# A read-back ring that takes its longest-unused place, one weight part a step earlier, and two splits moved ahead of weight conversions

## The chip, the cores and the metric

The kernel runs on one core of a Trainium2 chip. The metric is the device time of one execution in microseconds (us). Three timed runs of the kernel before gave 1104.66, 1105.78 and 1107.44 us, a median of 1105.78. The profile shown here is of a separate execution, which took 1105.05 us.

## The reference

An attention block with a computed position bias feeds two feed-forward layers. All data is fp32.

```python
attn  = softmax(q @ k.T / 8 + bias)          # 4 batches, 8 heads, 576 positions, head size 64
x     = attn @ v                             # 2304 tokens x 512
h     = x @ w_in;  x = (h - tanh(h)) @ w_out             # layer 0: 512 -> 2048 -> 512
h     = x @ w_in2; out = (s * relu(h)**2 + b) @ w_out2   # layer 1, the same sizes
```

## The kernel before

One core does the work of all 2304 tokens. PE multiplies, ACT (ScalarE) and DVE (VectorE) work on PSUM and SBUF tiles, POOL (GpSimd) does the elementwise work that is left, and SP issues nearly all DMAs. Each engine and SP's queue takes its instructions strictly in the order in which the program wrote them; an instruction that waits holds up all that stand behind it on its engine.

To keep fp32 accuracy every operand of a layer's product is a pair: a rounded high part (an ACT copy) and the low rest (a DVE or POOL subtraction). A product of two pairs is three matmuls. The program splits a hidden tile into such a pair in `split` (L383: ACT copy L385, DVE subtraction L386).

The program has these stages:

- The bias table, and then attention, up to about 280 us of the profile. The layer weights begin to be fetched and converted here.
- The chunk of layer 0: 512 tokens, in 16 steps n, one for each 128 rows of the hidden layer (loop at L839). Step n splits the hidden tile of step n-1, forms the first product of step n (`gemm1`, L369, 12 matmuls, into one of two PSUM tiles h), applies the gate (ACT L377, DVE L378) and adds the second product of step n-2 (`gemm2`, L610, 12 matmuls). So the first product of step n can't start before the split of step n-2 has read its tile h. Beside this, `weights_tick` converts two weights a step in a chain of POOL (L141), ACT (L142), DVE (L147, L152), ACT (L158) and POOL (L97). A list `xq` of small pieces prepares the tokens of the first block (ACT L769, DVE L772 and L775).
- Five blocks (`SUPER`, numbered q = 0 to 4; blocks 0 and 1 are of layer 0, the rest of layer 1). A block handles two column halves at once with a seven-product scheme: sums of weight quarters (`combine`, POOL L724), their split into pairs (`part`, three ACT casts L732 and four POOL subtractions L97) and the products (L912). In the first half-pass (eight steps p) a block forms the first products and adds the second products of one column half; in the second half-pass (16 turns, L999) it adds those of the other half, 12 matmuls (L610) a turn, from the second-layer weights alone.

The second-layer weights of layer 0 are 16 tiles of 512 KB, one for each f. They are kept in DRAM (`wsp_d`) and read back during blocks 0 and 1 through a ring of five SBUF places, w11 to w15 (`NR = 5`). The use order is fixed: each block uses f = 0 to 15 in its first half-pass and f = 15 to 0 in its second. That gives 64 turns, 0 to 63; block 1's second half-pass is turns 48 to 63. The plan of read-backs is made before the blocks are emitted (L676 to L684). Where a turn needs a tile that is in no place, the place whose tile is used again latest is overwritten; tiles that are never used again all have the same key, and Python's `max` then takes the first place of the dictionary:

```python
def next_use(x):
    return turns.index(ring_f[x], n) if ring_f[x] in turns[n:] else len(turns)
x = 16 - NR + n if n < 3 else max(ring_f, key=next_use)
```

`stream` (L686) emits a read-back (DMA L690) as soon as the turn that last uses the place has been emitted and one more turn begun, or at the latest at the turn that needs it. The DMA then waits on SP until PE is done with the place. Between the read-backs of block 1's second half-pass stand the DMAs of `renew` (L696), which fetch the 16 second-layer weights of layer 1, 256 KB each, for block 2.

Of the kernel before, what the change touches and what calls it, by code (L numbers as in the profile page):

```python
# [63 lines left out]
def tile_kernel(ctx, tc, qk, vd, wcat, wts, sb, ltab, psib, ipsi8, out):  # L64
# [55 lines left out]
    def fetch_more(ahead):  # L120
        while (k := len(fetched)) < min(32, wdone[1] + ahead) and all(j < wdone[1] for j in range(k) if fetched[j] == raw_tag(k)):
            fetch(k)
# [52 lines left out]
    def weights_tick():  # L175

        a, b_, c = wdone
        if c < b_:
            both(c)
            wdone[2] += 1  # L180
        if b_ < a:
            high(b_)
            low(b_)
            wdone[1] += 1
        if a in raw_w:
            begin(a, raw_w.pop(a))
            wdone[0] += 1
# [42 lines left out]
    with ExitStack() as c0:  # L230
# [62 lines left out]
        for n in range(NG + 2):  # L293
            if n < NG:
# [3 lines left out]
                for g in range(4 * G, 4 * G + 4):  # L298
                    hid = hids[g] = hp_.tile([128, LW], F32, tag="h", name="hid")
                    k = min(range(2), key=lambda k: held[k] + HC[k][0] + HC[k][1] * nd)  # L300
# [58 lines left out]
    def gemm1(c, f):  # L359
        layer, _, cn = CHUNKS[c]  # L360
        w = wt[layer * 16 + f, 0]
        h = hpool[0].tile([128, CH], F32, tag="h", name="h")[:, 0:cn]
        k = 0
        for kk in range(KD):
            wh = w[:, 0, kk * 128:kk * 128 + 128]
            wl_ = w[:, 1, kk * 128:kk * 128 + 128]
            xh, xl = x_t[c, kk]
            for a, x in ((wh, xh), (wh, xl), (wl_, xh)):
                nc.tensor.matmul(h, a, x, start=(k == 0), stop=(k == 3 * KD - 1))  # L369
                k += 1  # L370
        h_t[c, f] = h

    def gate(c, f):
        layer, _, cn = CHUNKS[c]
        h = h_t.pop((c, f))
        t = ring(F32)[:, 0:cn]
        nc.scalar.activation(out=t, in_=h, func=(AF.Tanh, AF.Relu)[layer])  # L377
        nc.vector.tensor_tensor(out=h, in0=h, in1=t, op=(ALU.subtract, ALU.mult)[layer])  # L378
        if layer:
            nc.vector.tensor_scalar(out=h, in0=h, scalar1=sb_t[:, 0:1], scalar2=sb_t[:, 1:2], op0=ALU.mult, op1=ALU.add)  # L380
        g_t[c, f] = (h, ring(F32R)[:, 0:cn], ring(F32R)[:, 0:cn])

    def split(c, f):  # L383
        g, gh, gl = g_t[c, f]
        nc.scalar.copy(gh, g)  # L385
        nc.vector.tensor_tensor(out=gl, in0=g, in1=gh.bitcast(F32), op=ALU.subtract)  # L386
# [209 lines left out]
    with ExitStack() as cb:  # L596
# [24 lines left out]
        def gemm2(c, f):  # L621
            layer, c0, cn = CHUNKS[c]
            _, gh, gl = g_t.pop((c, f))
            for d in range(KD):
                if f == 0:
                    acc[d] = ps_a.tile([128, 512], F32, tag=f"a{d}", name=f"a{d}")[:, 0:cn]
                accumulate(layer, acc[d], wt[f, 1], gh, gl, d, f == 0, f == NF - 1)
            if f == NF - 1:
                for d in range(KD):
                    leave(acc[d], layer, d, c0)  # L630
# [45 lines left out]
        turns = [f for _ in range(FIRST1) for f in (*range(NF), *reversed(range(NF)))]  # L676
        back, ring_f = [], {f: f for f in range(16 - NR, 16)}
        for n, f in enumerate(turns):
            if f not in ring_f.values():
                def next_use(x):  # L680
                    return turns.index(ring_f[x], n) if ring_f[x] in turns[n:] else len(turns)
                x = 16 - NR + n if n < 3 else max(ring_f, key=next_use)
                back.append((n, f, x, max([k for k in range(n) if turns[k] == ring_f[x]], default=-1)))
                ring_f[x] = f  # L684

        def stream(used):  # L686
# [18 lines left out]
        def load_w(q, p):  # L705
            if p >= NF // 2:
                q, p = q + 1, p - NF // 2
            if q < len(SUPER):
                if (q, p) not in wf_t:
                    wf_t[q, p] = place(f"w{4 - p}" if q == 0 and p < 2 else f"st{(p + 1) % 2}", [2, 512])  # L710
                nc.sync.dma_start(out=wf_t[q, p], in_=win_d[SUPER[q][0], 2 * p:2 * p + 2].rearrange("f p n -> p f n"))

        def combine(q, p):
            if p >= NF // 2:
                q, p = q + 1, p - NF // 2
            if q == len(SUPER):
                return
            w = wf_t[q, p]
            a11, a12, a21, a22 = (w[:, j // 2, j % 2 * 256:j % 2 * 256 + 256] for j in range(4))
            sums_ = sums_at[q, p] = place("XB", [4, 256])  # L720
            s2, s3, s1, s4 = (sums_[:, j] for j in range(4))
            for o, a, b, op in ((s1, a21, a22, ALU.add), (s2, s1, a11, ALU.subtract), (s3, a11, a21, ALU.subtract),
                                (s4, a12, s2, ALU.subtract)):
                nc.gpsimd.tensor_tensor(out=o, in0=a, in1=b, op=op)  # L724

        def part(q, p):
            w, sums_ = wf_t.pop((q, p)), sums_at.pop((q, p))
            cs = cs_t[q, p] = place(f"C{(p + q) % 2}", [7, 2, 256], F32R)
            groups = ((slice(4, 6), w[:, 0].rearrange("p (o n) -> p o n", o=2)), (slice(6, 7), w[:, 1:2, 256:512]),
                      (slice(0, 4), sums_))  # L730
            for o, x in groups:
                nc.scalar.copy(cs[:, o, 0], x)  # L732
            for o, x in groups[:2]:
                rest(cs[:, o, 1], x, cs[:, o, 0])
            for k in (0, 2):
                rest(cs[:, k:k + 2, 1], sums_[:, k:k + 2], cs[:, k:k + 2, 0])
# [102 lines left out]
        for n in range(NS):  # L839
            want = min(32, ND + max(0, int(RATE * (n - 2))))  # L840
            if n < 2:
                weights_tick()
            last = [seq[n - 1]] if len(PR) < n <= len(seq) else []
            while wdone[2] < want:
                weights_tick()
                if last:
                    split(*last.pop())
            if last:
                split(*last.pop())
            fetch_more(AHEAD)  # L850
            c, f = seq[n]
            if n >= len(PR):
                gemm1(c, f)
                gate(c, f)
            if n >= LAG:
                gemm2(*seq[n - LAG])
            for _ in range({8: 1, 9: 2, 10: 2, 11: 1, 12: 1, 13: 1, 14: 1, 15: 2}.get(n, 0)):
                xq.pop(0)()
            if n == 6:
                load_w(0, 0)  # L860
            if n == 9:
                combine(0, 0)
            if n == 12:
                part(0, 0)
                load_w(0, 1)
            if n == 14:
                combine(0, 1)
        flush(9)
        for _ in range(3):
            n, f, x, _ = back.pop(0)  # L870
# [210 lines left out]
```

## Time and profile before

| | |
|---|---|
| timed runs, median (lowest, highest) | 1105.78 us (1104.66, 1107.44) |
| profiled execution | 1105.05 us, span 1103.3 us |
| busy in the span | PE 95%, DVE 65%, ACT 53%, POOL 53% |
| mean granted TensorE clock | 0.975 of full speed |
| moved by DMA | 170.48 MB, 155 GB/s over the span |

The span runs from the first to the last instruction of the profiled execution; the 1.75 us between it and that execution's time lie outside the instructions. A line number is that of the kernel before. In a timeline row the first number is the start, the second how long the merged group of instructions lasted, and brackets hold the engine's idle time before it and what ended it. PE's matmuls overlap a little, so that starts, not ends, are compared. A windows row gives a stretch, its length, the busy us (and instructions) of PE, PEld, DVE, ACT and POOL, the granted clock as a share of full speed, the DMA engines' busy share and the GB/s moved. `x_d` stands for the DRAM tensors x1_d and x2_d, since the views leave numbers out of names.

### The profile page before, as it was taken

To read this page: it belongs to the slowest core of one execution; us is meant where nothing else is said; L and a number is where in the kernel's file an instruction comes from. 1 tells how busy PE (TensorE), PEld (TensorE's weight loads), DVE (VectorE), ACT (ScalarE), POOL (GpSimd) and SP (SyncE) were. 2 spreads that over 40 slices of the span, in tenths; PEclk is the share of its full clock that TensorE was granted. 3 is DMA by queue.
4 is the path that set the end of the run, shared out by engine and by line. 5 is a ranking of instruction groups with operands and counts; after the bars stand their busy time and mean duration, and the time that the engine had idled before them with its cause. 6 is when DMAs were issued, how large, how long until landed. Compare 5 with 4: busy or idle time off the path is not lost.

```text
span 1103.3 us, 18821 instructions
## 1 busy us (share of the span) xinstructions
PE 1049.0 (95%) x6664; PEld 846.6 (77%) x6664; DVE 720.7 (65%) x1415; ACT 584.7 (53%) x1208; POOL 589.8 (53%) x786
## 2 busy tenths in 40 slices
PE   9999999999999999999999955589999999999998
PEld 4366666666787799998888844489988999899987
DVE  8888888887487788877777721045565655755552
ACT  8887777777475545545444511045554443634441
POOL 2376777788387588516665300049941663355600
PEclk9999999999999999999999976699999999999999
DMA  7847474731696577685776322141121112021000
GB/s 284 308 159 268 160 262 143 223 133 61 227 366 257 189 274 291 210 286 179 250 249 212 132 96 86 57 144 59 58 86 49 57 50 84 29 86 40 20 29 29
DMA packets 68349, 170.48 MB, mean 155 GB/s; under 512 B 7456, under 2 KB 13728, under 8 KB 68256
## 3 DMA queue, kind: packets, MB, share of 16 engines
q1 hardware_dynamic: 67824, 168.89, 44.2%
q8 instruction: 52, 0.85, 0.3%
q10 hardware_dynamic: 432, 0.39, 0.1%
q14 instruction: 41, 0.34, 0.1%
HBM read 123.22 MB, written 46.04 MB: 153 GB/s over the span
## 4 chain that ended last, share of the span: by engine, by line
PE 76%; DMA 7%; DVE 6%; POOL 2%; issue 2%; ACT 2%; SPq 0%; DVEq 0%; ACTq 0%; POOLq 0%
PE a L610 19%; PE Z L912 8%; PE V L912 8%; PE o L533 6%; PE Y L912 6%; PE s L434 5%; PE X L912 5%; PE Z L610 5%; PE V L610 5%; DMA w<-wsp_d 4%; PE t L478 3%; PE X L610 3%; PE Y L610 2%; PE h L369 1%; POOL pn L472 1%
## 5 line engine op out<-in xcount | busy, mean ns | idle before, releaser
L97 POOL TENSOR_TENSOR C<-st,C 128x512 fp32r<-128x512 f32 x76 | 76.4, 1028 | 206.4 <-ACT C L732 167.3
L472 POOL TENSOR_SCALAR pn<-p,sm 128x576 f32<-128x576 f32 (+2 forms) x224 | 131.8, 605 | 41.4 <-DVE sm L463 37.8
L610 PE MATMUL a<-w,ring 128*128 128x512 f32 x576 | 146.5, 392 | 0.0
L610 PE MATMUL a<-ring,w 128*128 128x512 f32 (+1 forms) x576 | 127.7, 371 | 0.0
L610 PEld LDWEIGHTS a<-w,ring 128*128 128x128 f32 x576 | 107.5, 188 | 20.5
L610 PEld LDWEIGHTS a<-ring,w 128*128 128x128 f32 x576 | 105.8, 188 | 15.0
L441 DVE CUSTOM_DVE_ANT_0 raw<-s,bias 128x576 f32<-128x576 f32 x144 | 103.7, 752 | 17.4 <-PE s L434 15.5
L455 ACT ACTIVATE p<-raw,mn 128x576 f32<-128x576 f32 x144 | 110.9, 775 | 7.6 <-DVE mn L441 5.6
L97 POOL TENSOR_TENSOR C<-XB,C 128x512 fp32r<-128x512 f32 x80 | 107.2, 1363 | 0.0
L912 PE MATMUL Z<-C,C 128*128 128x384 f32 (+1 forms) x480 | 102.0, 346 | 1.1 <-DVE ring L825 0.7
L533 PE MATMUL o<-pt,vv 128*64 128x256 f32 (+1 forms) x640 | 95.0, 418 | 1.3 <-DVE xo L540 1.3
L434 PE MATMUL s<-qk 64*128 64x288 f32 (+1 forms) x640 | 91.6, 429 | 2.4 <-DVE mn L441 1.3
L912 PEld LDWEIGHTS Z<-C,C 128*128 128x128 f32 x480 | 85.4, 188 | 6.5 <-DVE ring L825 1.7
L434 PEld LDWEIGHTS s<-qk 64*128 64x128 f32 (+1 forms) x640 | 47.0, 175 | 43.3 <-DVE mn L441 18.8
L141 POOL TENSOR_SCALAR s<-w 128x512 f32<-128x512 f32 x60 | 48.4, 809 | 58.0 <-DMA w<-in_wts 25.8
L724 POOL TENSOR_TENSOR XB<-st 128x256 f32<-128x256 f32 x76 | 61.0, 802 | 19.5 <-DMA st<-win_d 17.4
L610 PE MATMUL X<-ring,w 128*128 128x384 f32 (+1 forms) x96 | 31.8, 447 | 38.0 <-DMA w<-wsp_d 38.0
L516 ACT COPY pt<-t 128x512 f32<-128x512 f32 x64 | 37.4, 584 | 45.0 <-PE c L478 28.6
L478 PEld LDWEIGHTS t<-ident,pn 64*128 64x128 f32 x1184 | 51.8, 139 | 9.3 <-DVE pt L516 1.5
L809 ACT ACTIVATE ring<-Y 128x384 f32<-128x384 f32 (+1 forms) x40 | 20.5, 513 | 70.7 <-PE Y L912 40.2
L533 PEld LDWEIGHTS o<-pt,vv 128*64 128x64 f32 x640 | 38.9, 136 | 24.1 <-DVE xo L540 1.7
L809 ACT ACTIVATE ring<-X 128x384 f32<-128x384 f32 (+1 forms) x40 | 20.5, 513 | 69.1 <-DVE X L931 35.6
(167 smaller groups left out, 2323.6 us busy)
## 6 DMA issues: line engine op xcount, KB each, us to landing
w<-in_wts SPq DMA_DIRECT2D x60, 512.0 KB, 4.9
w<-wsp_d SPq DMA_DIRECT2D x47, 512.0 KB, 4.7
st<-win_d SPq DMA_DIRECT2D x38, 512.0 KB, 3.8
qk<-in_qk SPq DMA_DIRECT2D x16, 864.0 KB, 5.8
bias_d<-m SPq DMA_DIRECT2D x36, 296.0 KB, 3.8
bias<-bias_d SPq DMA_DIRECT2D x32, 288.0 KB, 4.6
win_d<-s SPq DMA_DIRECT2D x32, 256.0 KB, 5.7
wsp_d<-w SPq DMA_DIRECT2D x16, 512.0 KB, 6.6
```

What stands on the lines that cost most here:

```text
L97: nc.gpsimd.tensor_tensor(out=lo, in0=raw, in1=hi.bitcast(F32), op=ALU.subtract)
L141: nc.gpsimd.tensor_scalar(out=sg, in0=hw, scalar1=0.0, scalar2=1.0, op0=ALU.mult, op1=ALU.mult)
L434: nc.tensor.matmul(o[0:n, c, 0:288], q[h, ee, t * 128:t * 128 + n], kk[h, ee], start=True, stop=True)
L441: nc.vector.tensor_tensor_reduce(out=raw.rearrange("p (c j) -> p c j", c=2), in0=s_t.pop((x, j))[:, :, 0:288], in1=bias_t[pairs[i][0], k]. ...
L455: nc.scalar.activation(out=p, in_=raw, func=AF.Exp, scale=-1.0, bias=mn, accum_out=sm[:, j:j + 1])
L472: nc.gpsimd.tensor_scalar(out=pn[:, c:c + b - a], in0=p[:, a:b], scalar1=sm[:, j:j + 1], scalar2=0.0, op0=ALU.mult, op1=ALU.add)
L478: nc.tensor.transpose(out_, in_, ident[ROWS[r], ROWS[r]])
L533: nc.tensor.matmul(o[h], v[:, e, j], unit_t[i, u][:, 8 if j == 4 else 4 * e + j, 0:n], start=(j == 0), stop=(j == 4))
L610: nc.tensor.matmul(o, x, y, start=first and j == 0, stop=last and j == 2)
L724: nc.gpsimd.tensor_tensor(out=o, in0=a, in1=b, op=op)
L809: nc.scalar.activation(out=t, in_=c, func=(AF.Tanh, AF.Relu)[layer])
L912: nc.tensor.matmul(o, cs[:, a, l, i * 128:i * 128 + 128], unit(q, u, i, r), start=begins and i == 0 and j == 0, stop=i == 1 and j == 2, sk ...
```

## The change

Three edits, in the order of the diff:

- The ring's key becomes a pair. Among places whose tiles are needed equally late, the one whose tile was last used longest ago is taken. Up to turn 52 no tie decides, so the plan differs only in the last 11 read-backs, turns 53 to 63. Before, all 11 go to w11, and each overwrites the tile used in the turn just before (turn 53: two turns before). Now they go to w15, w14, w12, w11, w13 in rotation, and the tile overwritten was last used five turns earlier (turn 53 takes w15, last used in turn 48).
- `part(0, 0)` and the load `load_w(0, 1)` that follows it move from the end of chunk step 12 to the end of chunk step 11.
- In chunk steps 13, 14 and 15 the split of the step before stands ahead of the step's weight conversions; before, it stood behind the first conversion. (Step 15 has no conversions, so two splits move.)

```diff
         for n, f in enumerate(turns):
             if f not in ring_f.values():
+                def last_use(x):
+                    return max([k for k in range(n) if turns[k] == ring_f[x]], default=-1)
+
                 def next_use(x):
-                    return turns.index(ring_f[x], n) if ring_f[x] in turns[n:] else len(turns)
+                    return turns.index(ring_f[x], n) if ring_f[x] in turns[n:] else len(turns), -last_use(x)
                 x = 16 - NR + n if n < 3 else max(ring_f, key=next_use)
-                back.append((n, f, x, max([k for k in range(n) if turns[k] == ring_f[x]], default=-1)))
+                back.append((n, f, x, last_use(x)))
                 ring_f[x] = f
...
             last = [seq[n - 1]] if len(PR) < n <= len(seq) else []
+            if n > 12:
+                split(*last.pop())
             while wdone[2] < want:
                 weights_tick()
                 if last:
...
-            if n == 12:
+            if n == 11:
                 part(0, 0)
                 load_w(0, 1)
```

In SP's queue during block 1's second half-pass stands, before (`w11` and the like are the SBUF places, `wsp_d` holds the read-back tiles, `wout_d` the weights of layer 1):

```order
L696 DMA w2_8493<-wout_d_72 128x512
L696 DMA w3_8513<-wout_d_72 128x512
L690 DMA w11_8536<-wsp_d_73 128x1024
L696 DMA w4_8538<-wout_d_72 128x512
L690 DMA w11_8558<-wsp_d_73 128x1024
L696 DMA w9_8560<-wout_d_72 128x512
L690 DMA w11_8580<-wsp_d_73 128x1024
```

and now:

```order
L699 DMA w1_8473<-wout_d_72 128x512
L693 DMA w14_8495<-wsp_d_73 128x1024
L699 DMA w2_8497<-wout_d_72 128x512
L693 DMA w12_8517<-wsp_d_73 128x1024
L699 DMA w3_8519<-wout_d_72 128x512
L693 DMA w11_8542<-wsp_d_73 128x1024
L699 DMA w4_8544<-wout_d_72 128x512
```

The read-backs rotate over the places and stand some three fetches of `renew` earlier in the queue; the number of DMAs is the same.

On DVE, from the gate of step 12 to the split of step 13 (tiles h are the hidden tiles, `ring_5685` and `ring_5754` the low parts that the splits write), stands before:

```order
L378 TENSOR_TENSOR h_5668<-h_5668,ring_5681 128x512
L775 TENSOR_TENSOR w5_5450<-w7_5575,w5_5450 128x384
L775 TENSOR_TENSOR w6_5452<-w8_5577,w6_5452 128x384
L147 SCALAR_TENSOR_TENSOR y_5665<-y_5665,s3_5664 128x512
L152 SCALAR_TENSOR_TENSOR s6_5663<-st1_5607,y_5665 128x512
L386 TENSOR_TENSOR ring_5685<-h_5668,ring_5684 128x512
L147 SCALAR_TENSOR_TENSOR y_5722<-y_5722,s2_5721 128x512
L152 SCALAR_TENSOR_TENSOR s0_5720<-w14_5609,y_5722 128x512
L378 TENSOR_TENSOR h_5737<-h_5737,ring_5750 128x512
L772 TENSOR_TENSOR w1_5700<-w5_5450,w1_5700 128x384
L772 TENSOR_TENSOR w2_5702<-w6_5452,w2_5702 128x384
L147 SCALAR_TENSOR_TENSOR y_5734<-y_5734,s3_5733 128x512
```

and now (the low parts are `ring_5695` and `ring_5754`):

```order
L378 TENSOR_TENSOR h_5678<-h_5678,ring_5691 128x512
L778 TENSOR_TENSOR w5_5450<-w7_5575,w5_5450 128x384
L778 TENSOR_TENSOR w6_5452<-w8_5577,w6_5452 128x384
L386 TENSOR_TENSOR ring_5695<-h_5678,ring_5694 128x512
L147 SCALAR_TENSOR_TENSOR y_5675<-y_5675,s3_5674 128x512
L152 SCALAR_TENSOR_TENSOR s6_5673<-st1_5607,y_5675 128x512
L147 SCALAR_TENSOR_TENSOR y_5724<-y_5724,s2_5723 128x512
L152 SCALAR_TENSOR_TENSOR s0_5722<-w14_5609,y_5724 128x512
L378 TENSOR_TENSOR h_5737<-h_5737,ring_5750 128x512
L775 TENSOR_TENSOR w1_5710<-w5_5450,w1_5710 128x384
L775 TENSOR_TENSOR w2_5712<-w6_5452,w2_5712 128x384
L386 TENSOR_TENSOR ring_5754<-h_5737,ring_5753 128x512
```

Each of the two splits moved past one pair L147, L152 of a weight conversion.

On POOL, around the end of step 11 (C0 is the tile that `part(0, 0)` fills, w12 and C3 are weights of the conversion chain), stands before:

```order
L141 TENSOR_SCALAR s3_5603<-st0_5541 128x512
L97 TENSOR_TENSOR w12_5645<-s6_5590,w12_5645 128x512
L141 TENSOR_SCALAR s2_5652<-w13_5543 128x512
L97 TENSOR_TENSOR C3_5530<-s0_5602,C3_5530 128x512
L141 TENSOR_SCALAR s3_5664<-st1_5607 128x512
L97 TENSOR_TENSOR C0_5704<-w4_5336,C0_5704 128x2x256
L97 TENSOR_TENSOR C0_5704<-w4_5336,C0_5704 128x256
L97 TENSOR_TENSOR C0_5704<-XB_5512,C0_5704 128x2x256 x2
```

and now:

```order
L141 TENSOR_SCALAR s3_5603<-st0_5541 128x512
L97 TENSOR_TENSOR C0_5645<-w4_5336,C0_5645 128x2x256
L97 TENSOR_TENSOR C0_5645<-w4_5336,C0_5645 128x256
L97 TENSOR_TENSOR C0_5645<-XB_5512,C0_5645 128x2x256 x2
L97 TENSOR_TENSOR w12_5655<-s6_5590,w12_5655 128x512
L141 TENSOR_SCALAR s2_5662<-w13_5543 128x512
L97 TENSOR_TENSOR C3_5530<-s0_5602,C3_5530 128x512
L141 TENSOR_SCALAR s3_5674<-st1_5607 128x512
```

The four subtractions of the part moved past two links of the conversion chain; on ACT the three casts L732 moved likewise, to directly behind the gate of step 11.

## Rows read from the trace of the kernel before

**Rows 1.** Waits of PE: line, releaser: us in total, times, longest.

```profile
PE X L610 <- DMA w<-wsp_d: 38.0, 11, 4.0
PE h L369 <- DVE ring L386: 4.1, 2, 3.1
```

**Rows 2.** Windows: chunk's last steps, block 0's second half-pass, block 1's unstalled, stalled turns.

```profile
350.62:367.70 17.08, 12.93 (x49) 10.18 (x49) 11.46 (x17) 5.96 (x12) 11.68 (x12) 0.90 0.43 156
466.34:499.78 33.44, 33.44 (x194) 33.44 (x194) 24.83 (x40) 13.84 (x30) 8.13 (x8) 1.00 0.68 237
620.66:634.26 13.60, 13.60 (x61) 11.07 (x59) 9.70 (x16) 5.32 (x11) 5.55 (x6) 1.00 0.50 161
634.26:724.63 90.37, 52.40 (x133) 37.76 (x133) 12.70 (x23) 9.76 (x20) 2.55 (x2) 0.72 0.23 79
```

**Rows 3.** Timeline of PE: block 1's second half-pass, first product of block 2.

```profile
620.66 0.84 PE L610 MATMUL X<-ring,w 128*128 128x512 f32 x3
623.38 0.84 PE L610 MATMUL X<-ring,w 128*128 128x512 f32 x3
...
642.24 1.62 PE L610 MATMUL X<-ring,w 128*128 128x512 f32 x3 [3.84 <-DMA w<-wsp_d]
...
724.63 1.20 PE L912 MATMUL X<-XA,C 128*128 128x384 f32 x6
```

**Rows 4.** Timeline of SP's queue: block 0's read-backs, then one stalled turn's DMAs.

```profile
472.19 17.55 SPq L690 DMA_DIRECT2D w<-wsp_d  x10
...
647.73 0.32 SPq L690 DMA_DIRECT2D w<-wsp_d  x1
648.10 0.42 SPq L696 DMA_DIRECT2D w<-wout_d  x1
```

**Rows 5.** Landing times: of all read-backs (line L690), of the fetches of renew.

```profile
DMA to landing us min/median/max: 3.3/4.7/6.9
...
w<-wout_d SPq DMA_DIRECT2D x16, 256.0 KB, 3.9
```

**Rows 6.** Timeline of PE: first products of steps 14, 15, and block 0's start.

```profile
351.62 3.01 PE L369 MATMUL h<-X,C 128*128 128x512 f32 x12 [1.01 <-DVE ring L386]
...
360.50 4.53 PE L369 MATMUL h<-X,C 128*128 128x512 f32 x12 [3.14 <-DVE ring L386]
...
367.70 1.23 PE L912 MATMUL X<-XA,C 128*128 128x384 f32 x6
...
378.86 0.62 PE L912 MATMUL V<-C,C 128*128 128x384 f32 x2 [0.22 <-DVE C L772]
```

**Rows 7.** Timeline of DVE: splits of steps 12 and 13, what stands between.

```profile
350.88 0.69 DVE L386 TENSOR_TENSOR ring<-h,ring 128x512 fp32r<-128x512 f32 x1 [2.58 <-ACT ring L385]
354.48 0.70 DVE L147 SCALAR_TENSOR_TENSOR y<-y,s 128x512 int32<-128x512 int32 x1 [2.91 <-POOL s L141]
...
356.42 2.10 DVE L772 TENSOR_TENSOR w<-w,w 128x384 fp32r<-128x384 f32 x2
358.44 0.68 DVE L147 SCALAR_TENSOR_TENSOR y<-y,s 128x512 int32<-128x512 int32 x1
...
359.76 0.68 DVE L386 TENSOR_TENSOR ring<-h,ring 128x512 fp32r<-128x512 f32 x1
```

**Rows 8.** Timeline of ACT and POOL: splits' copies, conversion's start, the part.

```profile
341.45 0.95 POOL L141 TENSOR_SCALAR s<-w 128x512 f32<-128x512 f32 x1
...
347.42 0.92 ACT L732 CAST C<-w 128x512 fp32r<-128x512 f32 x2
348.12 2.00 POOL L97 TENSOR_TENSOR C<-w,C 128x512 fp32r<-128x512 f32 x2 [2.23 <-ACT C L732]
...
350.06 2.53 POOL L97 TENSOR_TENSOR C<-XB,C 128x512 fp32r<-128x512 f32 x2
350.27 0.57 ACT L385 CAST ring<-h 128x512 fp32r<-128x512 f32 x1
...
356.54 0.59 ACT L385 CAST ring<-h 128x512 fp32r<-128x512 f32 x1
```

## The prediction

> **What bounds the kernel now.** I read the waits of PE first, since PE is busy 95% of the span. Two of them matter: 38.0 us in 11 waits for read-backs of `wsp_d`, and 4.1 us in 2 waits of a first product for a split [rows 1]. Then the windows, to see what these places cost beside the idle time. In block 1's second half-pass PE runs through its first five turns, 13.60 us of 13.60, and then needs 90.37 us for the other eleven, at a mean granted clock of 0.72, between its two levels of 1.2 and 2.4 GHz; DMA is busy to 0.23 there [rows 2]. The stalls cost more than their idle time: after each the matmuls themselves run slower. Third, the timelines: of PE for the length of a turn, of SP for what is issued when, and of DVE, ACT and POOL at the end of the chunk for why the two splits come late.
>
> **Edit 1, the ring.** It adds and removes no instruction; eleven read-backs get another place, and so another turn to wait for.
>
> An unstalled turn lasts 623.38 - 620.66 = 2.72 us; a stalled one (724.63 - 634.26) / 11 = 8.22 us [rows 2, 3]. The stalled turn is read-back and product in a row: the tile that the read-back overwrites was used in the turn just before, so its DMA can't go until that turn is done, and PE then waits 3.5 to 4 us for it (3.84 at 642.24) and works the rest, some 4.4 us, at the lowered clock.
>
> Now turn 53 overwrites a tile last used in turn 48, turn 54 one of turn 49, and so on: the DMA goes four turns, 4 x 2.72 = 10.9 us, before its tile is wanted. The landing time of all read-backs is 4.7 us in the median and 6.9 at most [rows 5], so 4.0 us of cover are left even for the slowest. Block 0's second half-pass is the nearest row: it has eleven read-backs with the same lead of four turns, its turns are shorter (33.44 / 16 = 2.09 us), ten of its read-backs go out in 17.55 us, and PE is busy 33.44 of 33.44 us at full clock [rows 2, 4].
>
> The queues that the read-backs are moved past: on SP each stands three fetches of `renew` earlier, and the first now stands ahead of the four stores of the finished accumulators. Those stores then start when turn 48 is done, near 623.4, and free the places of their SBUF copies some us later; the first split that such a place holds up is for turn 53, which starts at 634.26, so I cost it at nothing. If that cover were gone, each us of lateness would be a us of PE, once. The fetches of `renew` follow a read-back within 0.4 us, as at 647.73 and 648.10 [rows 4], with no wait of their own, and stay so.
>
> What is late next? Transport: the half-pass moves 161 x 13.60 + 79 x 90.37 = 9.3 MB [rows 2]. In 16 x 2.72 = 43.5 us that is 214 GB/s, under the 237 at which block 0's half-pass kept PE full. In its eleven loaded turns alone, however, a read-back and a fetch are 768 KB in 2.72 us, 289 GB/s; no row of these half-passes shows that. From the near side it costs nothing; from the far side, held to 237 GB/s, a turn would last 3.32 us and the eleven 6.6 us more. I take nothing: the lead of 10.9 us covers a lag that grows by 0.6 us a turn through all eleven but the last. Splits: DVE has 9.70 + 12.70 = 22.4 us of work in the whole half-pass and ACT 15.1 [rows 2], for 43.5 us.
>
> So the half-pass takes 43.5 us instead of 724.63 - 620.66 = 104.0: **-60.4 us**. Block 2 then starts as it does now: its own weights for the first steps are already there, and the last fetches of `renew` still wait for turns 61 to 63.
>
> **Edits 2 and 3, the end of the chunk.** From 350.62 to 367.70 PE has four products of 12 matmuls, 4 x 2.72 = 10.9 us of work, and takes 17.08 at a clock of 0.90 [rows 2]. The 6.2 us between are a wait of 1.0 at step 14, one of 3.14 at step 15, and a product that took 4.53 instead of 3.01 right after it [rows 6].
>
> Step 14 waits for the split of step 12. Its DVE half at 350.88 waited 2.58 us for its ACT half at 350.27, which stood behind the part's casts (from 347.42) and a conversion [rows 7, 8]. Step 15 waits for the split of step 13: its ACT half was done at 357.1, but DVE first did two token pieces (2.10 us) and a conversion pair (from 358.44) and reached it at 359.76 [rows 7, 8].
>
> I follow the new order with these durations. On POOL the part's four subtractions, 2.00 + 2.53 = 4.5 us [rows 8], now stand ahead of a conversion's start that ran at 341.45; it moves to about 345.5 (some of POOL's idle time takes up the rest), and DVE, which waits for it, is about 2.5 us later at the gate of step 12. From there the split of step 12 follows at once, without casts on ACT and conversion on DVE before it: it ends near 351.3, against 351.6 now. The wait at step 14 shrinks by 0.3 us only; what edit 3 gains there, edit 2 takes on POOL. Then the next two conversions find POOL earlier (DVE waited 2.91 us for it at 354.48 [rows 7], which goes), and the split of step 13 comes ahead of one: it ends at 357.0 to 358.0 instead of 360.4. The wait of 3.14 becomes 0 to 0.7, and with it the slow product. Block 0's first product would start at 363 to 364 instead of 367.70. Of these 4 us not all stays: ten us later PE waits for DVE's token pieces (378.86, [rows 6]), and DVE's own chain is only about 3 us earlier.
>
> Bounds: 6.2 us if all of the stretch's loss goes; below nothing, +2.5 us, if the delay by POOL reaches PE and nothing else does. I take **-3.0 us**, near where the replay with the rows' durations ends.
>
> The load behind the part (`load_w(0, 1)`) goes to SP ahead of two stores; nobody waits for either in these rows, so nothing.
>
> **Sum.** 1105.05 - 60.4 - 3.0 = 1041.6 us against the profiled execution. The median of the runs is 0.7 above that execution, so 1042.
>
> **Rivals.**
>
> A: transport sets the pace of the eleven turns. For it, 289 GB/s, which block 0's half-pass doesn't reach; against it, the lead and the DMA share of 0.68 at 237 GB/s. With 6.6 us more: 1049.
>
> B: a split becomes the late one. The DMA wait hid that ACT and DVE had whole turns idle. If each of the eleven turns waits 1 us for its split: 1053. Against it, block 0's half-pass again, where DVE worked 24.83 of 33.44 us and PE never waited.
>
> C: the change doesn't do what it says, because a read-back stands in SP's queue behind a fetch that waits for its own place. Each turn so hit stays at 8.2 us; three of eleven cost 16 us: 1058. Against it, no fetch waited [rows 4].
>
> D: slower. Two DMAs are in effect carried one after the other, and the stall now covers only one of them. A turn then costs a read-back and a fetch in a row, 4.7 + 3.9 = 8.6 us by the medians, and with the longest read-back 6.9 + 3.9 = 10.8 [rows 5]; it decides against the change once the pair takes more than today's 8.2 + 3.0 / 11 = 8.5 us. At 10.8: 11 x 2.6 = 28 us more than now, less 3, gives 1131. For it, the 79 GB/s of the stalled stretch; against it, that stretch moved little because little was asked for, and ten read-backs landing in 4.7 us went out 1.76 us apart without delay [rows 2, 4]. The Trainium skill's page "DMA: Bandwidth & Descriptors", section "Bandwidth", gives the rule that speaks for this rival: batch transfers to 1 MiB or more for three quarters of the peak, so 256 and 512 KB are on its poor side. By that page's cost of about 2.0 us plus bytes over 436 GB/s, read as one transfer after another, a turn would be an estimated 3.2 + 2.6 = 5.8 us and the kernel near 1076, still faster. The 237 GB/s of block 0's half-pass with 512 KB read-backs disagrees with that reading.
>
> **How the numbers follow.** The forecast has 0.84, A 0.09, B 0.03, C 0.02, D 0.02. The forecast's own range comes from the bounds of edits 2 and 3: 1105.8 - 60.4 - 6.2 = 1039 to 1105.8 - 60.4 + 2.5 = 1048. The range is 1038 to 1050, which takes in A at its full price and leaves out B, C and D. A measurement of this kernel can't tell less than 0.3%, 3.3 us, from no change. Every case but D is faster by ten times that; D lies on both sides of it. Faster 0.975, same 0.005, slower 0.02.
>
> **What would show it.** Right: in the waits of PE the row on `wsp_d` is gone or under 2 us; the second half-pass of block 1 is one stretch of 16 equal turns of 2.72 us at a granted clock of 1.0 and about 214 GB/s; the first products of steps 14 and 15 start about 6 us apart, and the second takes 3.0 us. Wrong: turns of 3.3 us with PE waiting for read-backs (A); PE waiting for ACT or DVE on `ring` (B); single turns of 8 us (C); landing times over 8 us (D); for edits 2 and 3, a DVE row L147 that waits for POOL near 344 by more than 2.5 us, or a wait of more than 1 us at step 15.

## The result and the profile after

The changed kernel takes 1039.87 us (median of four runs, 1038.54 to 1040.16). The four runs of the kernel before beside it have a median of 1105.49 us. The ratio is 0.9402 [0.9385, 0.9418], so the change takes off 65.6 us. The profiled execution took 1040.15 us, with a span of 1038.4 us and a mean granted clock of 1.000. PE is busy 99% of the span, DVE 69%, ACT 56%, POOL 57%.

The waits of PE in the changed kernel; the columns are those of [rows 1]:

```profile
PE b L239 <- POOL ident masks.py:199: 1.4, 1, 1.4
...
PE h L369 <- DVE ring L386: 0.9, 1, 0.9
```

The row on `wsp_d`, 38.0 us before, is gone altogether; the largest wait left is of the program's start, far from the change. Windows of the changed kernel, block 1's second half-pass (up to the start of block 2), and from there to the end:

```profile
616.21:659.73 43.52, 43.52 (x193) 36.04 (x192) 23.36 (x39) 15.03 (x30) 8.28 (x8) 1.00 0.71 247
659.73:1038.40 378.67, 374.37 (x1873) 337.63 (x1871) 209.06 (x367) 174.54 (x339) 187.38 (x194) 1.00 0.17 56
```

The first line answers to the last two of [rows 2] together. PE works 43.52 of 43.52 us at the upper clock, 2.4 GHz; before, the same 16 turns took 724.63 - 620.66 = 103.97. The second line is as long as the same stretch before, 1103.30 - 724.63 = 378.67 us: nothing is given back later.

The timeline of PE in the changed kernel: the first two turns of that half-pass and block 2's first product.

```profile
616.21 0.84 PE L610 MATMUL X<-ring,w 128*128 128x512 f32 x3
...
618.93 0.84 PE L610 MATMUL X<-ring,w 128*128 128x512 f32 x3
...
659.73 1.23 PE L917 MATMUL X<-XA,C 128*128 128x384 f32 x6
```

The starts are 2.72 us apart, as in the unstalled turns of [rows 3], now for all 16. The span's 64.9 us are thus 60.45 in the half-pass and 620.66 - 616.21 = 4.45 in its earlier start. Now SP's queue of the changed kernel (start, duration of the issue, line):

```profile
619.13 0.32 SPq L693 DMA_DIRECT2D w<-wsp_d  x1
...
620.23 2.74 SPq L173 DMA_DIRECT2D x_d<-ring  x4
...
623.77 0.57 SPq L693 DMA_DIRECT2D w<-wsp_d  x1
...
632.73 0.32 SPq L693 DMA_DIRECT2D w<-wsp_d  x1
633.10 0.42 SPq L699 DMA_DIRECT2D w<-wout_d  x1
635.45 0.32 SPq L693 DMA_DIRECT2D w<-wsp_d  x1
...
654.49 5.76 SPq L699 DMA_DIRECT2D w<-wout_d  x5
```

The read-back at 619.13 is for turn 53, which starts five turns after 616.21. The next one stood behind the four stores and went out at 623.77, about 2 us late. From 627.29 on a read-back goes out each 2.72 us with a fetch 0.4 us behind it. The last five fetches of `renew` now fall almost wholly into the half-pass. In the kernel before they went out behind it:

```profile
724.83 2.22 SPq L696 DMA_DIRECT2D w<-wout_d  x5
```

Landing times of all read-backs in the changed kernel, then of the eleven in the half-pass alone, in the changed kernel and in the kernel before:

```profile
DMA to landing us min/median/max: 3.5/5.4/7.8
...
DMA to landing us min/median/max: 3.8/4.7/6.6
...
DMA to landing us min/median/max: 3.3/3.5/3.8
```

The eleven lengthened from 3.5 to 4.7 us in the median and from 3.8 to 6.6 at most. A likely reason is that, with the read-backs issued ahead, more is in flight at once. The longest landings of all, 6.9 before [rows 5] and 7.8 now, are of other read-backs. The lead of 10.9 us covers the eleven, and so does the 8.8 us left to the one that went out at 623.77.

Last the chunk's end in the changed kernel: on PE the first products of steps 14 and 15 and the starts of block 0,

```profile
351.11 3.02 PE L369 MATMUL h<-X,C 128*128 128x512 f32 x12 [0.86 <-DVE ring L386]
...
356.70 2.90 PE L369 MATMUL h<-X,C 128*128 128x512 f32 x12
...
362.15 1.23 PE L917 MATMUL X<-XA,C 128*128 128x384 f32 x6
...
372.92 0.62 PE L917 MATMUL Z<-C,C 128*128 128x384 f32 x2 [0.77 <-DVE C L775]
```

and on DVE the conversion that POOL delays, the split of step 12, the token pieces and the split of step 13:

```profile
346.35 0.70 DVE L147 SCALAR_TENSOR_TENSOR y<-y,s 128x512 int32<-128x512 int32 x1 [2.38 <-POOL s L141]
...
350.37 0.69 DVE L386 TENSOR_TENSOR ring<-h,ring 128x512 fp32r<-128x512 f32 x1 [1.06 <-ACT ring L385]
...
354.82 1.10 DVE L775 TENSOR_TENSOR w<-w,w 128x384 fp32r<-128x384 f32 x2
355.84 0.68 DVE L386 TENSOR_TENSOR ring<-h,ring 128x512 fp32r<-128x512 f32 x1
```

The wait at step 14 is 0.86 us instead of 1.01, the one at step 15 is gone and with it the product of 4.53 us [rows 6]. DVE does wait for POOL behind the part's subtractions. The split of step 13 stands directly behind the token pieces. Those took 1.10 us, not 2.10 [rows 7]. Beside them POOL had an operation with one tile as input until 355.04, and then none until 356.13; in the kernel before it had this conversion's subtraction there:

```profile
356.71 1.39 POOL L97 TENSOR_TENSOR w<-s,w 128x512 fp32r<-128x512 f32 x1 [0.40 <-ACT w L158]
```

### The profile page after: what moved, and what is told of

It is laid out like the page before. It is cut to its first block, busy times and chain, and to the rows that moved or that the text cites. A ratio compares the mean times of both kernels' runs of the same rounds, so it can differ in the third digit from the quotient of the medians.

```text
span 1038.4 us, 18818 instructions
## 1 busy us (share of the span) xinstructions
PE 1024.7 (99%) x6664; PEld 832.8 (80%) x6664; DVE 721.6 (69%) x1415; ACT 584.8 (56%) x1208; POOL 592.2 (57%) x786
## 4 chain that ended last, share of the span: by engine, by line
PE 78%; DVE 7%; DMA 4%; POOL 3%; issue 2%; ACT 2%; SPq 0%; DVEq 0%; ACTq 0%; POOLq 0%
PE a L610 20%; PE Z L917 8%; PE V L917 8%; PE o L533 7%; PE s L434 6%; PE Y L917 6%; PE X L917 5%; PE V L610 5%; PE Z L610 5%; PE t L478 3%; PE Y L610 2%; PE X L610 2%; DVE raw L441 1%; POOL pn L472 1%; POOL C L97 1%
## 5 line engine op out<-in xcount | busy, mean ns | idle before, releaser
L478 PE MATMUL t<-ident,pn 64*128 64x64 f32 x1184 | 54.8, 223 | 1.0 <-DVE pt L516 1.0
```

What stands on the lines that cost most here:

```text
L478: nc.tensor.transpose(out_, in_, ident[ROWS[r], ROWS[r]])
```

## The experiments

### Each edit by itself

The ring's key alone, in the kernel before:

```diff
-return turns.index(ring_f[x], n) if ring_f[x] in turns[n:] else len(turns)
+return turns.index(ring_f[x], n) if ring_f[x] in turns[n:] else len(turns), -last_use(x)
```

> The kernel before with the ring's new key alone; the end of the chunk is as before. Theory T (each of the eleven stalled turns shrinks from 8.22 us to PE's own 2.72, and nothing else depends on it): block 1's second half-pass is 43.5 us long, 60.4 less, and the time is 1105.5 - 60.4 = 1045.1 us. The waits for split at the chunk's end, 1.0 and 3.14 us, stay. Rival R (the earlier end of the chunk helps the ring, or the ring's stretch gives back something later): more than 1 us away from 1045.

It took 1043.65 us (1042.41 to 1044.54), 0.9444 [0.9426, 0.9462] of the kernel before: 61.4 us less (59.4 to 63.4). PE with this edit alone, at the end of the chunk and around the half-pass:

```profile
351.57 4.61 PE L369 MATMUL h<-X,C 128*128 128x512 f32 x12 [2.22 <-DVE ring L386]
...
360.44 3.06 PE L369 MATMUL h<-X,C 128*128 128x512 f32 x12 [1.50 <-DVE ring L386]
...
618.43 0.84 PE L610 MATMUL X<-ring,w 128*128 128x512 f32 x3
...
661.95 1.23 PE L915 MATMUL X<-XA,C 128*128 128x384 f32 x6
```

The half-pass is 43.52 us without the other edits, so this one carries the result. The time is 1.45 us under the expected 1045.1, past the 1 us that the rival was given. Its interval covers 60.4 us, though, and the half-pass has the length that the theory says, so the rival isn't shown. In this profile the half-pass starts 620.66 - 618.43 = 2.23 us earlier with no edit ahead of it; so the 4.45 us of the changed kernel are not all the work of edits 2 and 3. The chunk is as in the kernel before, and yet its two waits are 2.22 and 1.50 us where [rows 6] have 1.01 and 3.14, and here the first product is the slow one. Between executions of the same instructions these waits scatter by more than a microsecond.

The part alone, and the splits alone:

```diff
-            if n == 12:
+            if n == 11:
                 part(0, 0)
                 load_w(0, 1)
```

> The kernel before with the part one step earlier and nothing else. Theory T (two causes in a row: the part's casts and a conversion delay the split of step 12, a conversion delays the split of step 13; POOL's four subtractions, moved ahead of the conversion chain, cost DVE about 2.4 us at the gate of step 12, but give the next conversions POOL earlier): the wait at step 14 grows to about 2 us, the one at step 15 shrinks to about 1, so that the slow product after it goes: 1.5 to 3 us faster than before, 1102.5 to 1104. Rival R (the part's move only costs, and the gain is the splits'): the wait at step 15 stays over 3 us and the time is 1105.5 or more.

```diff
+            if n > 12:
+                split(*last.pop())
             while wdone[2] < want:
```

> The kernel before with the two splits ahead of the conversions and nothing else. Theory T: the split of step 12 comes about 1 us earlier, so that the wait at step 14 goes, but POOL still does the part's four subtractions after it, DVE still waits for POOL at 354, and the split of step 13 ends near 359: a wait of about 3 us at step 15 stays, and the slow product with it. 1 to 1.5 us faster than before, 1104 to 1104.5. Rival R (the splits' move alone gives what both give): 4 us faster, 1101.4, no wait at step 15.

The part alone took 1102.48 us (1099.52 to 1105.23), ratio 0.9979 [0.9966, 0.9992]: 2.3 us less (0.9 to 3.8). PE with the part alone, first products of steps 13, 14 and 15:

```profile
346.46 3.02 PE L369 MATMUL h<-X,C 128*128 128x512 f32 x12 [1.03 <-DVE ring L386]
...
354.59 3.01 PE L369 MATMUL h<-X,C 128*128 128x512 f32 x12 [2.39 <-DVE ring L386]
...
360.81 3.03 PE L369 MATMUL h<-X,C 128*128 128x512 f32 x12 [0.48 <-DVE ring L386]
```

And DVE with the part alone:

```profile
348.75 0.70 DVE L147 SCALAR_TENSOR_TENSOR y<-y,s 128x512 int32<-128x512 int32 x1 [2.34 <-POOL s L141]
```

DVE waits 2.34 us for POOL, and behind it step 14 waits 2.39 us, more than in [rows 6]; step 13 waits too, which was not expected. At step 15 the wait shrinks from 3.14 to 0.48.

The splits alone took 1102.32 us (1101.4 to 1105.19), ratio 0.9984 [0.997, 0.9997]: 1.8 us less (0.3 to 3.3). PE with the splits alone, steps 14 and 15, and then DVE's wait for POOL:

```profile
349.97 2.92 PE L369 MATMUL h<-X,C 128*128 128x512 f32 x12
...
357.45 3.04 PE L369 MATMUL h<-X,C 128*128 128x512 f32 x12 [1.84 <-DVE ring L386]
```

```profile
353.84 0.70 DVE L147 SCALAR_TENSOR_TENSOR y<-y,s 128x512 int32<-128x512 int32 x1 [2.69 <-POOL s L141]
```

Step 14 no longer waits, and the wait for POOL at 353.84 stays, as in [rows 7]. Step 15 waits 1.84 us, and the slow product went, which was expected to stay.

Both together (the two diffs above, without the ring):

> The kernel before with the part and the splits moved, the ring as before. Theory T: the two moves together give 4 us or a little more, the difference between the time of the changed kernel and the ring's 60.4: 1105.5 - 4.5 = 1101.0; one wait under 1 us at step 14, none at step 15, full clock in block 0's first products; the eleven stalled turns stay at 8.2 us. Rival R (the difference of 5 us is scatter between runs or comes from the ring): the time stays within 1 us of 1105.5.

1101.78 us (1100.33 to 1106.32), ratio 0.9978 [0.9966, 0.9991]: 2.4 us less (1.0 to 3.8). That is less than the 4 us expected. PE's row on the splits in the profile of this version, an execution of 1106.32 us, the longest of the twelve:

```profile
PE h L369 <- DVE ring L386: 2.2, 2, 1.3
```

Each alone gives about what both give. A likely reason, from the rows above, is that the part's place costs at step 14 what the splits' place gains there. The intervals are too wide to rank the three versions, and the forecast of -3.0 us lies in the last one.

### How much lead a read-back needs

In the changed kernel's key, of the dead tiles the one used most recently, but at least two (or three) turns ago:

```diff
-..., -last_use(x)
+..., (last_use(x) <= n - 2) * (1 + last_use(x))
```

> The changed kernel, but in the last eleven read-backs the place overwritten is one last used two turns earlier (before: one; changed: five). The plan up to turn 52, the number of DMAs and the bytes are the same. Theory T (what counts is the time from the place's release to its next turn against the landing of one read-back): a read-back has one turn, 2.72 us, to land, and a release plus issue plus landing took about 3.8 us in the kernel before. Two read-backs overlap, so a turn takes about (2.72 + 3.8) / 2 = 3.3 us at full clock: PE waits about 0.5 us a turn, eleven turns cost 6 us, and the time is 1046; if the waits lower the clock, up to 1056. Rival R1 (any rotation is enough, since the fault was that only one read-back was under way): within 2 us of the changed kernel's 1039.9. Rival R2 (the pace is set by bytes, not by the lead): also as the changed kernel.

1047.96 us (1046.77 to 1048.47), ratio 0.949 [0.9476, 0.9504]. PE with a distance of two turns: the starts of five turns in a row, and the window from turn 52 to block 2.

```profile
644.20 0.94 PE L610 MATMUL X<-ring,w 128*128 128x512 f32 x3 [0.68 <-DMA w<-wsp_d]
...
647.34 0.93 PE L610 MATMUL X<-ring,w 128*128 128x512 f32 x3
...
651.48 0.94 PE L610 MATMUL X<-ring,w 128*128 128x512 f32 x3 [1.17 <-DMA w<-wsp_d]
...
654.33 0.84 PE L610 MATMUL X<-ring,w 128*128 128x512 f32 x3
...
658.13 0.93 PE L610 MATMUL X<-ring,w 128*128 128x512 f32 x3 [0.92 <-DMA w<-wsp_d]
```

```profile
627.29:667.43 40.14, 34.92 (x145) 26.27 (x144) 15.23 (x27) 11.17 (x22) 2.58 (x2) 1.00 0.56 190
```

Every second turn waits, 0.7 to 1.2 us, and two turns last 6.5 to 7.3 us: about one turn and the landing of a read-back (3.5 us in the median of these eleven), with two read-backs under way in turn. That is 40.14 / 12 = 3.3 us a turn, as expected from the lead; so a rotation of any kind (R1) is not enough. The granted clock stayed at 1.00 through these waits, while the stalls of 3.5 to 4 us had brought the stretch to 0.72 [rows 2].

```diff
-..., -last_use(x)
+..., (last_use(x) <= n - 3) * (1 + last_use(x))
```

> As the run before, with places last used three turns earlier. Theory T: a read-back has two turns, 5.4 us, to land, against a landing of 4.7 us in the median before and 5.4 in the changed kernel: three overlap, (2.72 + 3.8) / 3 = 2.2 us is under PE's 2.72, so no steady wait; single late ones (the longest landing was 7.8 us in the changed kernel) cost some tenths each: 1040 to 1043. Rival R3 (the whole lead of four turns is needed): over 1045.

1039.06 us (1038.69 to 1039.65), ratio 0.9411 [0.9397, 0.9425], which the changed kernel's interval covers. No wait for `wsp_d` is in the profile. Landing times of the eleven at this distance:

```profile
DMA to landing us min/median/max: 3.3/3.7/4.2
```

The DMA goes two turns, 5.44 us, ahead here; that covers even the longest of these landings, and PE waits for none. Two of the change's four turns of lead are spare.

### How far transport is from the pace

The changed kernel with an extra copy of 512 KB inside DRAM, which nothing uses, behind each of the last eleven read-backs:

```diff
+                if len(back) < 11:
+                    nc.sync.dma_start(out=junk_d[len(back)], in_=wsp_d[15 - len(back)])
```

> The changed kernel with one more 512 KB transfer, DRAM to DRAM, behind each of the last eleven read-backs; its result is used by nobody. A loaded turn then moves 1.25 MB (and writes half of it back to DRAM) instead of 768 KB: 482 GB/s at PE's pace. Theory T (bytes set the pace only above what the trace has shown, 365 to 380 GB/s): a turn would need about 3.5 us at 370 GB/s, 0.8 more than PE's, eleven of them 8.8 us; the lead of 10.9 us hides most of the lag that builds up, so PE waits 1 to 5 us in the last of the eleven turns and 1041 to 1046 us result. Rival R4 (transport was close to its limit already, and the changed kernel got by on its lead): 10 us or more slower than the changed kernel, over 1050, with waits from the third or fourth loaded turn on.

1043.53 us (1042.78 to 1046.12), ratio 0.9459 [0.9443, 0.9475], 3.7 us above the changed kernel and 4.5 above the version with a distance of three turns, which ran beside it. PE with the copies, three turns late in the half-pass, and windows of turns 51 to 56 and 57 to 62:

```profile
640.27 0.93 PE L611 MATMUL X<-ring,w 128*128 128x512 f32 x3
...
643.46 0.93 PE L611 MATMUL X<-ring,w 128*128 128x512 f32 x3 [0.21 <-DMA w<-wsp_d]
...
646.67 0.93 PE L611 MATMUL X<-ring,w 128*128 128x512 f32 x3 [0.23 <-DMA w<-wsp_d]
```

```profile
623.95:640.27 16.32, 16.32 (x73) 13.37 (x72) 11.83 (x22) 8.45 (x17) 0.00 (x0) 1.00 1.02 400
640.27:659.43 19.16, 17.92 (x74) 13.04 (x73) 5.57 (x9) 3.11 (x6) 2.58 (x2) 1.00 1.02 416
```

The DMA engines are full, at 400 to 416 GB/s. For six turns the lead still keeps PE at 2.72 us a turn (16.32 / 6); then transport sets 3.2 us a turn. This is what rival A would have looked like; the changed kernel itself, at 247 GB/s, is far from it.

### A second profile of the changed kernel, and the part split in two

The changed kernel again, without an edit:

> The changed kernel once more, beside the next run, so that both share the runs of the kernel before. 1039.9 us, within 1 us; the ratio to the kernel before within 0.938 to 0.942.

1039.86 us (1038.34 to 1042.9), ratio 0.9414 [0.9393, 0.9435]. PE in this second profile (of the execution of 1042.9 us), first products of steps 13 and 14:

```profile
346.85 3.01 PE L369 MATMUL h<-X,C 128*128 128x512 f32 x12 [1.00 <-DVE ring L386]
...
353.90 3.01 PE L369 MATMUL h<-X,C 128*128 128x512 f32 x12 [1.32 <-DVE ring L386]
```

The same program, with the median time unchanged, shows waits of 1.00 and 1.32 us where its first profile had none and 0.86; with a third they come to 2.6 us:

```profile
PE h L369 <- DVE ring L386: 2.6, 3, 1.3
```

The traces say where this difference begins. DVE's conversions (L152) write tiles `s` that are still being stored to `win_d`. Their waits for these stores, in the first profile and in the second:

```profile
DVE s L152 <- DMA win_d<-s: 0.8, 2, 0.5
...
DVE s L152 <- DMA win_d<-s: 3.9, 3, 2.6
```

All of them lie between 315 and 328 us, before the steps that edits 2 and 3 touch. Behind them the split of step 10 stands at 336.53 us in the first profile and at 339.37 in the second, 2.84 us later. The six profiles of kernels with both edits (the changed kernel's two, the two together, and the three with another lead or with copies) agree: the waits for stores are 0.8, 1.4, 2.5, 2.9, 3.1 and 3.9 us, and PE's waits for splits, in the same order, 0.9, 1.1, 2.2, 2.3, 2.3 and 2.6. No run changed the stores alone, so that they set PE's waits is likely, not shown.

Beside it, the part's ACT casts at the end of step 11 as in the change, but its POOL subtractions at the end of step 12:

```diff
             if n == 11:
-                part(0, 0)
+                part(0, 0, deferred)
                 load_w(0, 1)
+            if n == 12:
+                deferred.pop()()
```

> The changed kernel, with the part's three ACT casts left at the end of step 11 and its four POOL subtractions put back to the end of step 12. Theory T (edit 2 helps by taking the casts from before the split of step 12, and costs by putting POOL's 4.5 us ahead of the conversion that DVE waits for at the gate of step 12): DVE's wait for POOL of 2.4 us near 346 goes, the split of step 12 ends about 2 us earlier, the wait of 0.9 us at step 14 goes, and the time is 0.9 us or a little more below the changed kernel run beside it. Rival R5 (the conversions need POOL as early as edit 2 leaves it free; later subtractions hold up the conversion before step 15): a new wait of 1 us or more at step 15, the time the same or longer.

1039.16 us (1037.8 to 1039.86), ratio 0.9405 [0.9388, 0.9422]. PE with the part in two, first products of steps 14 and 15 and block 0's start:

```profile
348.71 2.88 PE L369 MATMUL h<-X,C 128*128 128x512 f32 x12
...
354.15 2.88 PE L369 MATMUL h<-X,C 128*128 128x512 f32 x12
...
359.59 1.23 PE L923 MATMUL X<-XA,C 128*128 128x384 f32 x6
```

Neither waits, and the waits of PE have no row of the first product on a split. DVE waits 1.0 us for the stores to `win_d` here, about as in the changed kernel's first profile. This is one profile, of the shortest of five executions (1037.8 us). In the median of the timed runs that is 0.7 us below the changed kernel beside it; the intervals overlap, so a gain in time isn't shown.

## Why the prediction was right

The time was forecast at 1042 us (range 1038 to 1050) and came out at 1039.87. By the prediction's steps:

- **Edit 1.** The term was -60.4 us; the half-pass gives -60.45, and the edit alone 61.4 (59.4 to 63.4). The mechanism is the one given. Of the 60.4 us, 38.0 were waits; the other 22 were matmuls that ran slower behind them at the lowered clock. Reading the length of the turns, instead of the waits alone, got both.
- **Cover.** 4.0 us were to be left for the slowest landing, 6.9 us of all read-backs; the slowest of the eleven took 6.6 us, which leaves 10.9 - 6.6 = 4.3 us. A DMA lead of two turns would have done, and one turn would have left 8 us of the gain unmade.
- **The stores that the first read-back passes**, costed at nothing: no turn of the half-pass waits for a place. They held up the second read-back by 2 us, which the forecast did not say; its cover took that up.
- **Transport.** 214 GB/s were forecast and 247 moved. What the byte sum left out are the last five fetches of `renew`, 5 x 256 KB = 1.3 MB. That they "still wait for turns 61 to 63" came true, since three of their places, w11, w13 and w15, are now in use up to turns 61, 62 and 63. Before, though, the first of the five waited for w11 up to turn 63 and held the others behind the half-pass; now it goes out behind turn 61, at 654.49. The 9.3 MB, read from the rows before, don't hold them. 9.3 and 1.3 MB in 43.52 us are 244 GB/s. It cost nothing. Rival A's 237 GB/s was no limit: with the copies 416 GB/s moved. These were transfers of 256 and 512 KB. The rule of the Trainium skill's page "DMA: Bandwidth & Descriptors", section "Bandwidth", to batch to 1 MiB or more for three quarters of the peak, did not bind them here, where several were in flight.
- **Edits 2 and 3.** The term was -3.0 us; the two alone measured -2.4 (-1.0 to -3.8). The forecast's parts of the stretch's loss (1.0, 3.14 and about 1.5 us) add up to 5.7 of the 6.2 us. The replay's details agree with the first profile: step 14 gains little (1.01 to 0.86), step 15's wait goes, DVE waits 2.38 us for POOL behind the part (forecast about 2.5), and the later wait for DVE's token pieces grows, from 0.22 [rows 6] to 0.77. The split of step 13 ends at 355.84 + 0.68 = 356.52, before the forecast's 357.0 to 358.0, since the token pieces ahead of it took 1.10 us and not 2.10. Block 0 starts 5.55 us earlier, more than forecast, and 1.1 us of that is given back before the half-pass (616.21 - 362.15 = 254.06 us between, against 620.66 - 367.70 = 252.96). Both kernels' waits here scatter between executions (0.9 and 2.6 us in two profiles of the changed kernel, 4.1 and 3.7 with the old chunk), so that a term of 3 us from one profile was near its own noise; the forecast named no such spread, and that -3.0 came so near -2.4 is partly luck.
- **Rivals.** B: no turn waits for ACT or DVE, with DVE busy 23.36 of 43.52 us. C: no turn of 8 us. D: a read-back and a fetch each 2.72 us cost PE nothing, so they are not carried one after the other. (Against D the forecast had block 0's ten read-backs 1.76 us apart, their whole stretch divided by ten; from the third on they went out 2.08 us apart, one a turn. That is still far under a landing, and the argument stands.)

Two small things stay open: why the stores to `win_d` take longer in one execution than in another, and whether the part in two is worth its 0.7 us. For the chunk without edits 2 and 3 the waits for these stores (1.2 us in the kernel before, 2.3 with the ring alone) don't explain PE's (4.1 and 3.7).

## What to carry to other kernels

Where a ring of buffers has several places that are dead, an equal key and Python's `max` pick the same one each time, and the transfer stands in line behind the work of the turn just before; break the tie by the oldest use, and the lead needs only to exceed the landing time (here two turns, 5.44 us, for landings of at most 4.2 us; one turn, 2.72 us, was too little). Read the landing times of the stage itself, not of all transfers of the line. Price a stall by the turn's whole length, since the work behind it ran slower too. Price microseconds at an engine's handover from more than one profile.

## What the runs showed of the hardware

- Repeated stalls of 3.5 to 4 us brought the granted clock over the stretch to 0.72 [rows 2]; waits of 0.7 to 1.2 us in every second turn left it at 1.00.
- Loads of 512 and 256 KB and 512 KB copies inside DRAM, issued from one queue, moved 400 to 416 GB/s together, at a DMA share of 1.02.
- A pair of DVE's two-input operations on 128x384 took 2.10 us with a subtraction of POOL beside it [rows 7], and 1.10 us in the changed kernel without one.
